# A linear attention, a top-2 expert layer and a gated layer on one core: other banks, other engines and other places for gathers

## The chip, the cores and the metric

The kernel runs on one core of a Trainium2 chip, as one program. The metric is the device time of a run in microseconds (us). The engines are TensorE (PE, matmuls; PEld its weight loads), VectorE (DVE), ScalarE (ACT), GpSimd (POOL) and SyncE (SP). In this kernel the matmuls write to PSUM, loads and the last stores are issued by SP, other stores by ACT, and gathers by a list of indices by POOL.

## The reference

```python
q_s = softmax(q, over its 64 columns);  k_s = softmax(k, over the 576 positions)
attn = q_s @ (k_s.T @ v)                       # 8 batches x 8 heads
x = attn as 4608 tokens x 512
noisy = x @ w_gate + log1p(exp(x @ w_noise)) * noise
top2 of 8 experts per token, weights = softmax of the two
x = sum over the two: weight * (relu(x @ w1[e]) @ w2[e])   # 512 -> 1024 -> 512
out = (((x @ m1) * (x @ m2)) @ w3) @ w_out
```

All values are float32. A product of two float32 values is made of three matmuls, since each operand is split in a high and a low part.

## The kernel before

**Attention and routing (`front`, L142).** A generator that handles 36 tiles of 128 tokens. Per tile `q_sub` (DVE maximum, POOL subtraction), `q_tr` (PE transpose), `q_exp` (ACT), `q_mm` (PE into the PSUM tile `pm`, 4 KB per partition, one buffer), `q_out` (DVE `qr`, ACT `xn` from `pm`, DVE `lp`, POOL `xt`, SP stores it to X). Between them `k_step` works on the keys of the next batch. `route` makes places and lists for groups of tokens: `onehots` (L371) turns a place into a tile number `jf` and a position `pf` (five DVE instructions), compares them with a ramp (`oa`, `ob`, DVE), multiplies `ob` by the token's tag (L402, POOL) and sums over PE. While the front is alone, its transposes take turns in four PSUM tiles of 2 KB (pools `ptr` and `pyy`, two each, called banks here), and the routing has two of its own (`phh`). At the mark "A" the first list `idxa` is there, and the experts' products start; from then on the rest of the front is drawn in between them (`hook_front`).

**Expert layer.** Work goes by units: a unit is two or three tiles of 128 gathered tokens of one expert. `product1` (eight PSUM tiles `ph`, each evacuated by ACT L738 and DVE L739 into `hT`) is followed by `product2` (a PSUM tile `py` for each 128 tokens; ACT L749 copies it to `y`, ACT issues the store to Y, L751). The tokens of the next unit are gathered by POOL from X, and turned by `transp`: in units 0 to 2 by a copy on POOL (`xr`, L122) and PE transposes, later by DVE alone. Unit 2 is the first whose gathers are cut in quarters (L137); the list of its indices is made at the end of unit 1. Until L872 a scheduler sets the order of instructions on each engine, by costs of its own; from there on the order is that of the code. Each engine works through its own queue in order.

**Last expert and gated layer.** `columns` (L877) after unit 5 prepares the places of every token: a clamp of `pos` on DVE (L879), then PE copies them to all partitions (`replicate`). Every tile of the gated layer needs two rows of Y per token, fetched by `gather2` (eight gathers on POOL) into the four buffers of `g2p`, weighted by ACT (L957) and DVE (L960) in `take`, and turned. `take` also starts the gather of the tile two further on. Tiles 0 and 1 are gathered before the last two units; `take(0)` to `take(2)` stand within these two units (events, L974 to L976), so gathers from Y are issued there between the stores to Y. The framework lets a store to Y wait for gathers from Y that stand before it in the code, and a gather wait for stores before it. The gated layer then runs 12 blocks of three tiles.

Of the kernel before, what the change touches and what calls it, by code (L numbers as in the profile page):

```python
# [24 lines left out]
D = NH * DH  # L25
# [13 lines left out]
CFB = {1: 0, 5: 1, 8: 2}  # L39
GROUPS = [(0, 9), (9, 15), (15, 18), (18, 26), (26, 32), (32, 35), (35, 36)]  # L40
# [3 lines left out]
def moe_chain_kernel(ctx, tc, q, kt, v0, v1, noise, wg, w1, w2, mw1, mw2, mw3t, mwo, out):  # L44
# [40 lines left out]
    def open_late():  # L85
        early.close()
        for name, bufs in (("w2", 4), ("ht", 1), ("xt", 2), ("xg", 3), ("y", 2)):
            late[name] = pool(main, name + "p", bufs, side="right", reuse_waits="tile")
    ptr = pool(main, "ptr", 2, space=PSUM)
    phh = pool(main, "phh", 2, space=PSUM)  # L90
    pyy = pool(main, "pyy", 2, space=PSUM)

# [9 lines left out]
    turns = {"ph": [phh], "py": [pyy]}  # L102
# [11 lines left out]
    def transp(src, xt, t, quarters):  # L114
        if quarters:
            pt = extra["xq"].tile([128, 4, 4, 32], F32, name="xq", tag="xq")
            V.transpose(out=pt, in_=src.rearrange("p (j c d) -> p c j d", j=4, c=4))  # L117
            pt = pt.rearrange("p c j t -> p c (j t)")
        else:
            pt = ptr.tile([128, 4, 128], F32, name="pt", tag="pt")  # L120
            rows = late["y"].tile([128, 4, 4, 32], F32, name="xr", tag="y")
            G.tensor_copy(out=rows, in_=by_chunk(src))  # L122
            for c in range(4):
                P.transpose(pt[:, c, :], rows[:, c].rearrange("p i d -> p (i d)"), ident)
        split(pt, xt[:, 0, :, 128 * t:128 * t + 128], xt[:, 1, :, 128 * t:128 * t + 128])
# [16 lines left out]
    def front(st):  # L142
# [12 lines left out]
        def bank(shape, route=False):  # L155
            if alone[0]:
                if route:
                    return phh.tile(shape, F32, name="rb", tag="ph")
                alone[1] += 1
                pl, tg = ((ptr, "pt"), (pyy, "py"))[alone[1] % 2]  # L160
                return pl.tile(shape, F32, name="fb", tag=tg)
            alone[1] += 1
            if alone[1] % 3 == 0:
                return pyy.tile(shape, F32, name="rb", tag="py")
            return ptr.tile(shape, F32, name="pt", tag="pt")
# [176 lines left out]
        def q_mm(i):  # L342
            pms[i] = pm = pmm.tile([128, 4, 256], F32, name="pm", tag="pm")
            b0, b1 = (i * 128) // S, (i * 128 + 127) // S
            for p in range(4):
                if b0 == b1:
                    P.matmul(pm[:, p, 0:162], eqs[i][:, p, :], tab[b0 % 3][:, p, :], start=True, stop=True)
                else:
                    P.matmul(pm[0:64, p, 0:162], eqs[i][:, p, 0:64], tab[b0 % 3][:, p, :], start=True, stop=True)
                    P.matmul(pm[64:128, p, 0:162], eqs[i][:, p, 64:128], tab[b1 % 3][:, p, :], start=True, stop=True)  # L350
# [20 lines left out]
        def onehots(i0, sl, cols, acc):  # L371
            n, kk = sl.shape[1], sl.shape[2]
            si = sm.tile([128, n, kk], I32, name="si", tag="si")
            V.tensor_copy(out=si, in_=sl)
            yield
            sj = sm.tile([128, n, kk], I32, name="sj", tag="sj")
            V.tensor_single_scalar(out=sj, in_=si, scalar=7, op=ALU.arith_shift_right)
            V.tensor_single_scalar(out=si, in_=si, scalar=127, op=ALU.bitwise_and)
            yield
            jf = sm.tile([128, n, kk], F32, name="jf", tag="jf")  # L380
            V.tensor_copy(out=jf, in_=sj)
            pf = sm.tile([128, n, kk], F32, name="pf", tag="pf")
            V.tensor_copy(out=pf, in_=si)
            yield
            per = 4 // kk
            for c0 in range(0, n, 2 * per):
                c1 = min(n, c0 + 2 * per)
                pl = bank([128, cols], True)
                for a in range(c0, c1, per):
# [11 lines left out]
                    obn = ob[:, 0:m].rearrange("p (n k) c -> p n k c", k=kk)  # L401
                    G.tensor_tensor(out=obn, in0=obn, in1=tag[:, i0 + a:i0 + z][:, :, None, None].to_broadcast(  # L402
                        [128, z - a, kk, cols]), op=ALU.mult)
# [26 lines left out]
        def route(gi):  # L430
# [32 lines left out]
            pr = bank([128, n, E], True)  # L463
# [51 lines left out]
            if i1 in (HT, NT):  # L515
                pc = bank([128, E], True)
# [201 lines left out]
    def xpose(u, t):  # L718
        if t == 0:
            xts[u] = late["xt"].tile([128, 2, 4, 384], F32R, name="xT", tag="xT")  # L720
        transp(xg.pop((u, t)), xts[u], t, u > na)
# [155 lines left out]
    def columns():  # L877

        V.tensor_scalar(out=pos, in0=pos, scalar1=float(E * ROWS - 1), scalar2=None, op0=ALU.min)  # L879
# [65 lines left out]
    def gather2(i):  # L945
        if i >= NT:
            return
        for k in range(2):
            y = extra["g2"].tile([128, D], F32, name="yg", tag="yg")
# [3 lines left out]
    def take(i):  # L953
# [11 lines left out]
        transp(y0, xts["g", b], t, True)  # L965
        gather2(i + 2)
# [6 lines left out]
    events[nu - 3, 7] = [w34_begin]  # L973
    events[nu - 2, 9] = [lambda: take(0)]  # L974
    events[nu - 1, 2] = [lambda: take(1)]
    events[nu - 1, 7] = [lambda: take(2), load_b]  # L976
    for u in range(na, nu):
# [4 lines left out]
        if u == na:  # L982
            turns["py"].append(ptr)
        if u == na + 3:
# [3 lines left out]
    for j in range(4):  # L988
        wscratch(("w", j), 20 + j, late["w2"])

    most = nc.values_load(nmax[0:1, 0:1], min_val=0, max_val=T)

    def gated():
# [3 lines left out]
        for b in range(nblk):  # L997
            xt = xts.pop(("g", b))
            pT = late["ht"].tile([128, 2, 8, 384], F32R, name="hT", tag="hT")
            for fb in range(8):  # L1000
# [13 lines left out]
                if b + 1 < nblk and fb in CFB:  # L1014
                    take(BT * (b + 1) + CFB[fb])
            for m in range(BT):
# [9 lines left out]
                if b + 1 < nblk and m + 8 in CFB:  # L1026
                    take(BT * (b + 1) + CFB[m + 8])

# [127 lines left out]
```

## Time and profile before

| | us |
|---|---|
| median of 3 runs (1743.0 to 1746.36) | 1745.32 |
| the profiled run | 1746.65 |
| its span, first to last instruction | 1744.7 |
| PE busy in it | 1665.7 |
| DVE / POOL / ACT busy | 886.3 / 690.7 / 572.5 |

The profile is of one execution. Its tables give busy time per engine, the span in slices with the clock that TensorE was granted (1.00 is 2.4 GHz, 0.50 is 1.2 GHz), what ended each idle time, and, for a chosen stretch, the instructions in order of time.

### The profile page before, as it was taken

What the parts mean: (1) busy time and instruction counts of PE and PEld (TensorE: products, weight loads), DVE (VectorE), ACT (ScalarE), POOL (GpSimd) and SP (SyncE); (2) the same over time, 40 slices, a digit from 0 to 9 for tenths busy, and PEclk for the clock granted to TensorE, in tenths of its full rate; (3) what the DMA queues carried; (4) which work ended last, traced back from release to release, by engine and by line L of the source; (5) the groups of instructions that cost most, each with busy time, mean ns of one, the idle gap of its engine ahead of it and who ended that gap; (6) DMA issues with size and microseconds to landing.
All of it is one profiled execution on the core that took longest, in us unless ns stands there. A gap on an engine that the chain in (4) does not pass through costs nothing. (4 is left out here: it accounts for less than half of the span.)

```text
span 1744.7 us, 26430 instructions
## 1 busy us (share of the span) xinstructions
PE 1665.7 (95%) x9903; PEld 1519.5 (87%) x9903; DVE 886.3 (51%) x2251; ACT 572.5 (33%) x1195; POOL 690.7 (40%) x706
## 2 busy tenths in 40 slices
PE   6887979989999999999999999899999999999998
PEld 5666868988989989899998988789999999999997
DVE  6699735766567575774767513233323233332321
ACT  6553322333233333332333312232223233232321
POOL 4456334414334143341443420544454454444500
PEclk9898989999999999999999999999999999999999
DMA  8875344535355253553545484521111111111100
GB/s 297 263 238 173 110 151 150 175 104 168 112 169 172 86 177 124 162 157 104 166 152 173 154 318 165 187 101 43 49 53 48 52 54 35 44 48 52 50 23 20
DMA packets 130060, 221.51 MB, mean 127 GB/s; under 512 B 18560, under 2 KB 65792, under 8 KB 126848
## 3 DMA queue, kind: packets, MB, share of 16 engines
q1 hardware_dynamic: 95040, 152.07, 26.7%
q0 software_dynamic: 19072, 39.88, 8.4%
q10 hardware_dynamic: 15808, 27.71, 4.3%
q8 instruction: 85, 1.39, 0.3%
q14 instruction: 55, 0.45, 0.1%
HBM read 152.22 MB, written 67.37 MB: 126 GB/s over the span
## 5 line engine op out<-in xcount | busy, mean ns | idle before, releaser
L98 PE MATMUL ph<-xT,w 128*128 128x384 f32 (+1 forms) x1792 | 576.2, 322 | 13.6 <-DVE hT L739 9.4
L99 PE MATMUL ph<-xT,w 128*128 128x384 f32 (+1 forms) x1792 | 574.6, 321 | 0.8 <-DVE xT L95 0.7
L100 PE MATMUL ph<-xT,w 128*128 128x384 f32 (+1 forms) x1792 | 574.0, 320 | 0.0
L137 POOL DMA_INDIRECT xg<-X,idxq x288 | 282.5, 981 | 467.7 <-DVE xq L117 395.3
L137 POOL DMA_INDIRECT yg<-Y,posq x288 | 295.0, 1024 | 364.9 <-DVE yg L960 209.0
L98 PEld LDWEIGHTS ph<-xT,w 128*128 128x128 f32 x1792 | 339.8, 190 | 18.6 <-DVE hT L739 11.8
L100 PE MATMUL py<-w,hT 128*128 128x512 f32 x904 | 353.0, 390 | 0.4
L99 PE MATMUL py<-w,hT 128*128 128x512 f32 x904 | 352.3, 390 | 0.0
L98 PE MATMUL py<-w,hT 128*128 128x512 f32 x904 | 352.2, 390 | 0.0
L99 PEld LDWEIGHTS ph<-xT,w 128*128 128x128 f32 x1792 | 339.4, 189 | 3.3 <-DVE xT L95 1.5
L100 PEld LDWEIGHTS ph<-xT,w 128*128 128x128 f32 x1792 | 339.5, 189 | 0.0
L100 PEld LDWEIGHTS py<-w,hT 128*128 128x128 f32 x904 | 169.7, 188 | 37.4 <-DVE hT L739 2.0
L99 PEld LDWEIGHTS py<-w,hT 128*128 128x128 f32 x904 | 169.7, 188 | 34.0
L98 PEld LDWEIGHTS py<-w,hT 128*128 128x128 f32 x904 | 169.7, 188 | 33.9
L1012 DVE TENSOR_TENSOR a<-a,ph 128x384 f32<-128x384 f32 x96 | 53.0, 552 | 281.6 <-PE ph L100 263.5
L739 DVE SCALAR_TENSOR_TENSOR hT<-ph,hT 128x256 fp32r<-128x256 f32 (+1 forms) x256 | 120.5, 474 | 103.4 <-ACT hT L738 100.4
L738 ACT ACTIVATE hT<-ph 128x256 fp32r<-128x256 f32 (+1 forms) x256 | 107.2, 426 | 158.1 <-PE ph L100 143.6
L95 DVE TENSOR_TENSOR xT<-xq,xT 128x512 fp32r<-128x512 f32 x108 | 74.8, 693 | 154.9 <-ACT xT L94 154.9
L749 ACT COPY y<-py 128x512 f32<-128x512 f32 x77 | 45.2, 587 | 258.0 <-PE py L100 214.4
L94 ACT CAST xT<-xq 128x512 fp32r<-128x512 f32 x108 | 67.0, 620 | 138.7 <-DVE xq L117 129.2
L94 ACT CAST hT<-a 128x384 fp32r<-128x384 f32 x96 | 49.4, 514 | 182.3 <-DVE a L1012 182.3
L95 DVE TENSOR_TENSOR w<-raw,w 128x1024 fp32r<-128x1024 f32 x72 | 88.8, 1236 | 11.7 <-ACT w L94 11.6
(203 smaller groups left out, 1529.5 us busy)
## 6 DMA issues: line engine op xcount, KB each, us to landing
raw<-in_w_dram SPq DMA_DIRECT2D x72, 512.0 KB, 4.1
w<-WS SPq DMA_DIRECT2D x24, 1024.0 KB, 6.6
WS<-hl SPq DMA_DIRECT2D x80, 256.0 KB, 2.8
Y<-y ACTq DMA_DIRECT2D x77, 256.0 KB, 2.5
k<-in_kt_dram SPq DMA_DIRECT2D x32, 288.0 KB, 4.4
q<-in_q_dram SPq DMA_DIRECT2D x36, 256.0 KB, 4.0
X<-xt SPq DMA_DIRECT2D x36, 256.0 KB, 2.4
out_dram<-y SPq DMA_DIRECT2D x36, 256.0 KB, 2.1
```

Of the source, the lines that this page charges most:

```text
L94: A.copy(out=hi, in_=src)
L95: V.tensor_tensor(out=lo, in0=src, in1=hi.bitcast(F32), op=ALU.subtract)
L98: P.matmul(ps, st_h, mv_h, start=first, stop=False)
L99: P.matmul(ps, st_h, mv_l, start=False, stop=False)
L100: P.matmul(ps, st_l, mv_h, start=False, stop=last)
L137: G.indirect_dma_start(out=dst[:, 128 * j:128 * j + 128], out_offset=None, in_=src[:].rearrange("t (i c) -> (t i) c", i=4), in_offset=bass ...
L738: A.activation(out=hT[:, 0, fb, :N], in_=ph[:, :N], func=AF.Relu)
L739: V.scalar_tensor_tensor(out=hT[:, 1, fb, :N], in0=ph[:, :N], scalar=0.0, in1=hT[:, 0, fb, :N].bitcast(F32), op0=ALU.max, op1=ALU.subtract)
L749: A.copy(out=by_chunk(y), in_=py.rearrange("p (c i d) -> p c i d", c=4, i=4))
L1012: V.tensor_tensor(out=a, in0=a, in1=ps, op=ALU.mult)
```

## The change

- PSUM: the two banks of `phh` are opened only when the expert layer starts; until then they hold `pm2`, a second tile for `q_mm`, which takes `pm` and `pm2` in turn. The routing's tiles join the four banks of the transposes.
- `onehots`: three float instructions on DVE instead of five with integers; the tags are multiplied by ACT, one instruction for each tile of tokens (54 in all), instead of by POOL (25).
- `transp` in units 0 to 2: the copy `xr` is made by ACT (units 0 and 1) or DVE (unit 2) instead of POOL.
- The clamp of `pos` moves from `columns` to the end of unit 2.
- `gather2(2)` moves ahead, to the middle of the last unit but one, into a freed weight buffer `raw`; `gather2(3)` and `gather2(4)` move behind the last store to Y; the first gated block takes its turns later (`CF0`).

```diff
+CF0 = {4: 0, 7: 1, 9: 2}
...
     def open_late():
         early.close()
+        turns["ph"].append(pool(main, "phh", 2, space=PSUM, side="right", reuse_waits="tile"))
...
-    phh = pool(main, "phh", 2, space=PSUM)
     pyy = pool(main, "pyy", 2, space=PSUM)
+    pm2 = pool(early, "pm2", 1, space=PSUM, side="right")
...
-    def transp(src, xt, t, quarters):
-        if quarters:
+    def transp(src, xt, t, straight):
+        if straight is None:
...
-            G.tensor_copy(out=rows, in_=by_chunk(src))
+            straight(out=rows, in_=by_chunk(src))
...
-        def bank(shape, route=False):
+        def bank(shape):
             if alone[0]:
-                if route:
-                    return phh.tile(shape, F32, name="rb", tag="ph")
...
-            pms[i] = pm = pmm.tile([128, 4, 256], F32, name="pm", tag="pm")
+            pms[i] = pm = (pm2 if alone[0] and i % 2 else pmm).tile([128, 4, 256], F32, name="pm", tag="pm")
...
-            si = sm.tile([128, n, kk], I32, name="si", tag="si")
-            V.tensor_copy(out=si, in_=sl)
-            yield
-            sj = sm.tile([128, n, kk], I32, name="sj", tag="sj")
-            V.tensor_single_scalar(out=sj, in_=si, scalar=7, op=ALU.arith_shift_right)
-            V.tensor_single_scalar(out=si, in_=si, scalar=127, op=ALU.bitwise_and)
-            yield
+
             jf = sm.tile([128, n, kk], F32, name="jf", tag="jf")
-            V.tensor_copy(out=jf, in_=sj)
+            V.tensor_scalar(out=jf, in0=sl, scalar1=1.0 / 128, scalar2=-0.49609375, op0=ALU.mult, op1=ALU.add)
+            yield
+            V.tensor_scalar(out=jf, in0=jf, scalar1=8388608.0, scalar2=-8388608.0, op0=ALU.add, op1=ALU.add)
+            yield
             pf = sm.tile([128, n, kk], F32, name="pf", tag="pf")
-            V.tensor_copy(out=pf, in_=si)
+            V.scalar_tensor_tensor(out=pf, in0=jf, scalar=-128.0, in1=sl, op0=ALU.mult, op1=ALU.add)
...
-                    obn = ob[:, 0:m].rearrange("p (n k) c -> p n k c", k=kk)
-                    G.tensor_tensor(out=obn, in0=obn, in1=tag[:, i0 + a:i0 + z][:, :, None, None].to_broadcast(
-                        [128, z - a, kk, cols]), op=ALU.mult)
+                    for j in range(z - a):
+                        obj = ob[:, kk * j:kk * j + kk]
+                        A.mul(out=obj, in_=obj, mul=tag[:, i0 + a + j:i0 + a + j + 1])
...
-        transp(xg.pop((u, t)), xts[u], t, u > na)
+        transp(xg.pop((u, t)), xts[u], t, None if u > na else V.tensor_copy if u == na else A.copy)
...
     def columns():
 
-        V.tensor_scalar(out=pos, in0=pos, scalar1=float(E * ROWS - 1), scalar2=None, op0=ALU.min)
...
+        if i == 2:
+            raw = rawp.tile([128, 2, D], F32, name="raw", tag="raw")
         for k in range(2):
-            y = extra["g2"].tile([128, D], F32, name="yg", tag="yg")
+            y = raw[:, k] if i == 2 else extra["g2"].tile([128, D], F32, name="yg", tag="yg")
...
-        gather2(i + 2)
+        if i >= BT:
+            gather2(i + 2)
...
+    events[nu - 2, 4] = [lambda: gather2(2)]
     events[nu - 2, 9] = [lambda: take(0)]
...
             turns["py"].append(ptr)
+            V.tensor_scalar(out=pos, in0=pos, scalar1=float(E * ROWS - 1), scalar2=None, op0=ALU.min)
...
         wscratch(("w", j), 20 + j, late["w2"])
+    gather2(3)
+    gather2(4)
...
+            turn_at = CFB if b else CF0
...
-                if b + 1 < nblk and fb in CFB:
-                    take(BT * (b + 1) + CFB[fb])
+                if b + 1 < nblk and fb in turn_at:
+                    take(BT * (b + 1) + turn_at[fb])
```

ACT's queue at the end of the last unit but one (steps 8 to 10 of unit `nu - 2`), before; `DMASW` are the signals of POOL's gathers, `DMAHW` those of other DMAs.

```order
L751 DMA Y_59<-y_12742 128x512 [waits DMAHW3_49,Activation_49]
L957 ACTIVATE yg_12363<-yg_12363,gwq_3515 128x128 x4
L94 CAST xT_12753<-xq_12754 128x4x128 [waits DVE_49]
L749 COPY y_12793<-py_12768 128x4x4x32 [waits DMAHW2_49,PE_49]
L751 DMA Y_59<-y_12793 128x512 [waits DMASW4_49,DMASW5_49,DMASW3_49,DMASW6_49,DMASW2_49,DMASW7_49,DMASW1_49,DMAHW5_49,DMASW0_49,Activation_49]
L738 ACTIVATE hT_12796<-ph_12797 128x256 [waits PE_49]
```

The same place in the changed kernel.

```order
L748 DMA Y_59<-y_12744 128x512 [waits DMAHW3_49,Activation_49]
L955 ACTIVATE yg_12356<-yg_12356,gwq_3508 128x128 x4
L96 CAST xT_12755<-xq_12756 128x4x128 [waits DVE_49]
L746 COPY y_12785<-py_12760 128x4x4x32 [waits DMAHW2_49,PE_49]
L748 DMA Y_59<-y_12785 128x512 [waits Activation_49]
L735 ACTIVATE hT_12788<-ph_12789 128x256 [waits PE_49]
```

The store of the third tile no longer waits for any gather; the instructions around it are the same.

POOL's queue from the end of unit 1 on, before (`xg` from `idx` are unit 2's gathers, those from `idxq` the next units').

```order
L402 TENSOR_TENSOR ob<-ob,tag 128x160 x2
L709 DMA xg<-X,idx 128x512 x3
L122 COPY xr<-xg 128x512
L137 DMA xg<-X,idxq 128x128 x4
L122 COPY xr<-xg 128x512
L137 DMA xg<-X,idxq 128x128 x4
L122 COPY xr<-xg 128x512
L137 DMA xg<-X,idxq 128x128 x40
```

DVE's queue in the changed kernel, where the three copies now stand: the end of unit 1 and the first evacuation of unit 2.

```order
L736 SCALAR_TENSOR_TENSOR hT<-ph,hT 128x256
L124 COPY xr<-xg 128x512 x2
L97 TENSOR_TENSOR xT<-pt,xT 128x4x128 x2
L124 COPY xr<-xg 128x512
L97 TENSOR_TENSOR xT<-pt,xT 128x4x128
L736 SCALAR_TENSOR_TENSOR hT<-ph,hT 128x384
```

The copies left POOL, where four gathers stood between each two of them, and stand on DVE with only the evacuations of the same tiles between.

DVE's queue between unit 5 and unit 6, before: conversion of the gated layer's weights (L628 to L635), then `columns`.

```order
L645 TENSOR_TENSOR hl<-mf,u 128x256
L628 TENSOR_SCALAR ex<-cr 128x256
L630 TENSOR_SCALAR b_4790<-cr 128x256
L633 SCALAR_TENSOR_TENSOR b_4790<-cr,b_4790 128x256
L635 SCALAR_TENSOR_TENSOR mf<-ex,b_4790 128x256
L879 TENSOR_SCALAR pos<-pos 128x72
L880 TENSOR_SCALAR posq<-py,quart 128x288
```

The same place in the changed kernel.

```order
L642 TENSOR_TENSOR hl<-mf,u 128x256
L625 TENSOR_SCALAR ex<-cr 128x256
L627 TENSOR_SCALAR b_4784<-cr 128x256
L630 SCALAR_TENSOR_TENSOR b_4784<-cr,b_4784 128x256
L632 SCALAR_TENSOR_TENSOR mf<-ex,b_4784 128x256
L876 TENSOR_SCALAR posq<-py,quart 128x288
```

The clamp of `pos` (L879) is gone from here; it now stands at the end of unit 2.

## Rows read from the trace of the kernel before

**Rows 1.** The page, busy time of each engine over the span.

```profile
PE 1665.7 (95%) x9903; PEld 1519.5 (87%) x9903; DVE 886.3 (51%) x2251; ACT 572.5 (33%) x1195; POOL 690.7 (40%) x706
```

**Rows 2.** Windows, end of unit 5 to product2 of unit 6; a later product1.

```profile
368.10:393.45 25.35, 20.63 (x161) 20.46 (x161) 17.73 (x42) 9.00 (x16) 3.78 (x4) 0.87 0.49 146
487.35:504.58 17.23, 17.15 (x98) 16.82 (x96) 14.34 (x31) 9.01 (x16) 3.77 (x4) 1.00 0.60 191
```

**Rows 3.** Windows: unit 5, last unit, gated blocks 0 and 1.

```profile
345.90:368.10 22.20, 22.20 (x145) 19.97 (x143) 11.10 (x30) 6.31 (x14) 6.45 (x7) 1.00 0.27 82
...
1130.56:1185.08 54.52, 51.62 (x265) 48.47 (x264) 16.17 (x34) 14.81 (x34) 26.62 (x27) 0.97 0.32 113
1185.08:1235.38 50.30, 50.30 (x266) 47.44 (x265) 16.26 (x34) 14.91 (x34) 24.81 (x25) 1.00 0.17 48
1099.39:1130.56 31.17, 24.17 (x146) 22.08 (x145) 7.97 (x20) 7.37 (x20) 19.36 (x20) 0.89 0.58 210
```

**Rows 4.** Timeline of ACT, last two units: start, length, in brackets idle before.

```profile
1089.32 0.33 ACTq L751 DMA_DIRECT2D Y<-y  x1
...
1111.26 0.94 ACT L738 ACTIVATE hT<-ph 128x256 fp32r<-128x256 f32 x3 [11.08 <-DMA yg<-Y,posq]
...
1140.22 0.58 ACT L749 COPY y<-py 128x512 f32<-128x512 f32 x1 [14.32 <-DMA yg<-Y,posq]
```

**Rows 5.** Timeline of POOL and DVE, last two units.

```profile
1104.31 0.94 POOL L137 DMA_INDIRECT yg<-Y,posq  x1 [0.30 <-issue]
...
1070.12 1.23 DVE L95 TENSOR_TENSOR w<-raw,w 128x1024 fp32r<-128x1024 f32 x1 [0.38 <-ACT w L94]
```

**Rows 6.** Chain of waits: start, length, the last gather's landing.

```profile
1133.78 5.91 DMA yg<-Y,posq
```

**Rows 7.** Timeline of PE between units 5 and 6.

```profile
372.83 1.19 PE L132 MATMUL py<-pos,ident 128*32 128x72 f32 x32 [4.72 <-DVE pos L879]
```

**Rows 8.** Timelines of POOL, ACT, DVE and PE between units 1 and 2.

```profile
248.10 0.61 POOL L122 COPY xr<-xg 128x512 f32<-128x512 f32 x1 [12.63 <-DMA Y<-y]
...
249.46 0.59 ACT L94 CAST xT<-pt 128x512 fp32r<-128x512 f32 x1 [0.62 <-PE pt L124]
...
250.08 0.69 DVE L95 TENSOR_TENSOR xT<-pt,xT 128x512 fp32r<-128x512 f32 x1 [9.36 <-ACT xT L94]
...
248.76 0.66 PE L124 MATMUL pt<-ident,xr 128*128 128x128 f32 x4 [0.55 <-POOL xr L122]
254.38 1.12 PE L124 MATMUL pt<-ident,xr 128*128 128x128 f32 x4 [4.96 <-POOL xr L122]
...
261.79 0.69 PE L98 MATMUL ph<-xT,w 128*128 128x384 f32 x1 [0.68 <-ACT xT L94]
```

**Rows 9.** Windows of the front: alone, start of the products, units 0 and 1.

```profile
62.00:130.00 68.00, 54.04 (x560) 45.53 (x560) 60.94 (x249) 41.97 (x91) 32.63 (x34) 0.95 0.76 247
130.00:153.40 23.40, 15.93 (x154) 12.83 (x150) 21.44 (x42) 7.74 (x13) 18.77 (x20) 0.72 0.70 222
153.40:248.90 95.50, 88.81 (x680) 77.52 (x681) 69.07 (x279) 32.05 (x68) 34.45 (x38) 1.00 0.40 138
```

**Rows 10.** Waits from 40 to 153: engine, releaser, us in total, times, longest.

```profile
PE pm L347 <- DVE lp L360: 12.7, 8, 4.0
...
DVE qr L355 <- PE pm L347: 7.3, 8, 1.4
```

**Rows 11.** Groups by line, 60 to 153.4, DVE and POOL: busy, mean ns.

```profile
L377 DVE TENSOR_SCALAR sj<-si 128x12 int32<-128x12 int32 (+3 forms) x6 | 2.2, 361 | 0.0
...
L402 POOL TENSOR_TENSOR ob<-ob,tag 128x320 f16<-128x320 f16 (+4 forms) x10 | 6.7, 673 | 4.9 <-DVE ob L398 2.4 <-DVE si L374 1.4 <-DVE qr L355 0.9
```

**Rows 12.** Timeline of DVE, one instruction at two times.

```profile
89.24 0.15 DVE L269 TENSOR_SCALAR ks<-ks 128x4 f32<-128x4 f32 x1
...
135.09 3.25 DVE L269 TENSOR_SCALAR ks<-ks 128x4 f32<-128x4 f32 x1
```

**Rows 13.** Waits from 153 to 249.

```profile
POOL ob L402 <- DVE ob L398: 19.1, 8, 8.3
```

More of the change, by code (lines that the diff above doesn't have):

```diff
@@ L100, in mm3 @@
         P.matmul(ps, st_l, mv_h, start=False, stop=last)
-    turns = {"ph": [phh], "py": [pyy]}
+    turns = {"ph": [], "py": [pyy]}
     def bank_of(kind, shape):
@@ L372, in onehots @@
             n, kk = sl.shape[1], sl.shape[2]
-            si = sm.tile([128, n, kk], I32, name="si", tag="si")
-            V.tensor_copy(out=si, in_=sl)
+            jf = sm.tile([128, n, kk], F32, name="jf", tag="jf")
+            V.tensor_scalar(out=jf, in0=sl, scalar1=1.0 / 128, scalar2=-0.49609375, op0=ALU.mult, op1=ALU.add)
             yield
-            sj = sm.tile([128, n, kk], I32, name="sj", tag="sj")
-            V.tensor_single_scalar(out=sj, in_=si, scalar=7, op=ALU.arith_shift_right)
-            V.tensor_single_scalar(out=si, in_=si, scalar=127, op=ALU.bitwise_and)
+            V.tensor_scalar(out=jf, in0=jf, scalar1=8388608.0, scalar2=-8388608.0, op0=ALU.add, op1=ALU.add)
             yield
-            jf = sm.tile([128, n, kk], F32, name="jf", tag="jf")
-            V.tensor_copy(out=jf, in_=sj)
             pf = sm.tile([128, n, kk], F32, name="pf", tag="pf")
-            V.tensor_copy(out=pf, in_=si)
+            V.scalar_tensor_tensor(out=pf, in0=jf, scalar=-128.0, in1=sl, op0=ALU.mult, op1=ALU.add)
             yield
@@ L387, in onehots @@
                 c1 = min(n, c0 + 2 * per)
-                pl = bank([128, cols], True)
+                pl = bank([128, cols])
                 for a in range(c0, c1, per):
@@ L462, in route @@
             yield
-            pr = bank([128, n, E], True)
+            pr = bank([128, n, E])
             P.matmul(pr, upper, m, start=True, stop=False)
@@ L515, in route @@
             if i1 in (HT, NT):
-                pc = bank([128, E], True)
+                pc = bank([128, E])
                 P.matmul(pc, onesb, run, start=True, stop=True)
@@ L964, in take @@
             xts["g", b] = late["xt"].tile([128, 2, 4, 384], F32R, name="xT", tag="xT")
-        transp(y0, xts["g", b], t, True)
-        gather2(i + 2)
+        transp(y0, xts["g", b], t, None)
+        if i >= BT:
+            gather2(i + 2)
     def load_b():
@@ L1025, in gated @@
                 nc.sync.dma_start(out=out[r:r + 128, :], in_=y)
-                if b + 1 < nblk and m + 8 in CFB:
-                    take(BT * (b + 1) + CFB[m + 8])
+                if b + 1 < nblk and m + 8 in turn_at:
+                    take(BT * (b + 1) + turn_at[m + 8])
     gated()
```

## The prediction

> **What bounds the kernel now.** I read the busy times of the page first: PE is busy 1665.7 of 1744.7 us [rows 1]. The change leaves the number of matmuls as it is, so it can win only where PE stands (79 us in all) or runs at the lower clock. Next the slices, to find these places, and windows cut at them. Three lie in the experts' part and one is the front. Between unit 5 and unit 6, 25.35 us pass until product1 is over, at a mean clock of 0.87; the same product1 elsewhere takes 17.23 [rows 2]. The last unit takes 31.17 us and the first gated block 54.52, where equal work takes 22.20 and 50.30 [rows 3]. Between units 1 and 2, PE has only transposes to do for 13 us [rows 8]. In the front DVE is the fullest engine: 60.94 of 68 us while the front is alone, 21.44 of 23.4 until the products start; after that PE is, 88.81 of 95.5 [rows 9]. Last I read at each place what ended the wait, and then the queues of the change there.
>
> **The stores to Y.** In the last unit but one, `take(0)` issues `gather2(2)` ahead of the third store to Y, and this store waits for it. Eight gathers at 0.94 + 0.30 us make 9.9 us [rows 5], and the landing follows. ACT's queue is in order, so behind the store stand the evacuations of the last unit's product1: ACT is idle 11.08 us, until the gathers' data is there, and again 14.32 us behind the first store of the last unit [rows 4]. PE runs out of PSUM tiles. Price: 31.17 - 22.20 = 8.97 us and 54.52 - 50.30 = 4.22 us, together 13.2; both windows show a mean clock below 1, 0.89 and 0.97, so the sum holds the half clock after the stalls too [rows 3].
> In the changed kernel `gather2(2)` waits for a weight buffer, which is free when its split is done: 1070.12 + 1.23 = 1071.4 on the clock of the profile, if it is the first of this unit's splits [rows 5]. Then 9.9 us of issue and at most 5.9 of landing (the longest that I see [rows 6]) end at 1087.2, ahead of the first store to Y at 1089.3 [rows 4]. If the buffer is that of the fourth split, three `ph` tiles of 2.15 us (17.23 / 8) later, ACT is held 4.4 us inside product2; a `py` tile takes PE (50.30 - 2 x 17.23) / 3 = 5.3 us, and four of them take turns: nothing. No gather stands between the later stores.
> What is late next are `gather2(3)` and `gather2(4)`, which wait for the last store. Let T be the start of the gated layer. The copy of 0.58 and the store end by T + 0.6 + 0.3 + 5.9 = T + 6.8, sixteen gathers of 1.24 are issued by T + 16.7 and T + 26.6, and landed by T + 22.6 and T + 32.5. A gated block's first part is two times the 17.23 of rows 2; `take(3)` stands after five eighths of it, T + 21.5, `take(4)` at its end, T + 34.5. In the worst case ACT is 1.1 us late at the first, and PE has four `ph` tiles to bridge that. So I take the whole 13.2; bounds 9 (the first stall alone) and 13.2.
>
> **The clamp of the places.** PE stands 4.72 us for the clamp of `pos` [rows 7], which queues on DVE behind weight conversions. The 25.35 us hold a product1 (17.23) and two copies of the places, 2 x 0.8 us at full clock (the 1.19 of the row is at half clock). The rest, 25.35 - 17.23 - 1.6 = 6.5 us, is stall and half clock. The clamp now stands three units earlier; PE's copies wait only for banks, and `posq` and `gwq` are read much later. The conversions now hold DVE beside unit 6's first tile, which four `ph` tiles hide. I take 6.5; bounds 4.7 and 6.5.
>
> **The copies between units 1 and 2.** POOL makes `xr` at 248.10 when a store to Y has landed, and then issues four gathers before each further copy: PE's second transposes start at 254.38, unit 2 at 261.79 [rows 8]. On DVE no gather stands between. The first copy starts at 248.10 as before and takes at most the 0.69 of DVE's row. Transposes 0.66 to 249.45; the second copy waits for them, 250.1; transposes 250.8; ACT 0.59 to 251.4, DVE 0.69 to 252.1; third copy 252.8; transposes at half clock 1.12 to 253.9; ACT to 254.5. Unit 2 starts at 254.6 instead of 261.79: 7.2 us. [...] Bounds: 5 (each copy waits for a further store of 2 us) and 7.5. The conversions' first load is tied to unit 2's first tile, and the stop that it makes later moves along.
>
> **The front.** Four effects, none of which the trace shows alone.
> The integer steps: ten calls drop two DVE instructions each, six calls by 153. At 0.15 us free of POOL [rows 12] to 0.36 [rows 11] that is 1.8 to 4.3 us of DVE; I take 3.
> The second `pm`: DVE waited 7.3 us for PE's `pm`, and PE 12.7 for DVE to empty it [rows 10]. DVE is the fuller engine, so 0 to 7.3; DVE needs the time for other work in most of them, I take 2.5.
> POOL's multiplications: 6.7 us by 153 [rows 11]. A DVE instruction of 0.15 us took 3.25 beside POOL's work [rows 12], so taking some away frees DVE: 0 to 6.7, I take 2.5.
> Against it: ACT gets 54 small multiplications and five copies. None is longer than the 0.59 of a 128x512 row, so at most 35 us of ACT, of which the front alone has 42 of 68 busy and units 0 and 1 32 of 95.5 [rows 9]. Their waits are worse than their work: POOL waited 19.1 us for `ob` in units 0 and 1 [rows 13], and ACT has evacuations queued behind. The routing now shares four banks. Below nothing is excluded, as both only add waits; from 0 to 19, and I take 2, near the low end, since PE then has the front's own matmuls between the products.
> Front: 3 + 2.5 + 2.5 - 2 = 6 us, bounds +18 (gains all, cost none: 4.3 + 7.3 + 6.7) and -17.
> By the Trainium skill (SBUF — State Buffer, Who interferes with whom), DVE and GpSimd share a pair of ports that whoever comes first holds for its whole instruction; rows 12 agree with it. By that rule all 6.7 us would come back, and the front would win 10.
>
> **Edits that cost nothing.** The later turns of the first block (`CF0`) only move work inside a block in which PE is full; `ph`'s later opening leaves PE's order in the experts as it is. The last block's end is untouched.
>
> **Sum.** 13.2 + 6.5 + 7.2 + 6 = 32.9 us off the profiled run's 1746.65 gives 1713.7. The median of the runs shown is 1.3 lower than the profiled one, so 1712.4.
>
> **Rivals.**
> The front frees DVE fully (17 in 100): +18 instead of 6, 1700. For it: DVE is 90% full there. Against it: `xn` and `xt` have one buffer each, and loads keep the DMA share at 0.76 [rows 9].
> The front wins nothing, or loses up to 15 us, by waits in ACT's queue (16 in 100): 1718 to 1733, some 1724 in the middle.
> The gathers' stall comes back (4 in 100): `gather2(3)` lands late by more than four `ph` tiles cover, as 5.91 us is from a stretch with fewer weights loading. From T + 30 on each us counts in full; with the 13.2 lost, 1725.6.
> Slower (3 in 100): ACT takes over POOL's waits in units 0 and 1. The place is ACT's queue ahead of L738, with two `ph` tiles there. If the 19.1 us and all 35 us of new work delayed PE, the front would lose 54 instead of winning: 1746.65 - 26.9 + 54 - 1.3 = 1772. It decides from 27 us of such delay on. Against it: ACT is idle for two thirds of that stretch.
>
> **How the numbers follow.** Forecast 60 in 100, alone 1706 to 1718. The range takes in the bounds of the front and most of the rivals: 1697 to 1730. About 0.2% (3.5 us) is what a measurement can tell; only the last rival and the worst of the second end there or above. Faster 0.95, within it 0.02, slower 0.03.
>
> **What would show it.** The stores: no ACT idle time ended by a gather from Y in the last two units, and these at 22.2 and 50.3 us. The clamp: no PE wait for `pos`, product1 over within 19 us of unit 5's end. The copies: unit 2 starts within 6 us of unit 1's end. The front: unit 0's first product before 150 us, and PE's idle time in units 0 and 1 not above 6.7 us. It is wrong if ACT shows waits for `ob` with PE idle behind them, or if the first gated block still takes over 52 us.

## The result and the profile after

The changed kernel takes 1722.72 us (median of 4 runs, 1715.42 to 1725.67) against 1744.73 us before: ratio 0.9868, 95% interval 0.9835 to 0.9900. A second group of runs gave 0.9831 (0.9809 to 0.9853). It is faster by 22 to 27 us, where I had forecast 32.9 off the profiled run. The profiled run's span is 1721.8 us, 22.9 under that of before.

The page first: PE has the same work as in [rows 1] in a shorter span, POOL has less, ACT more.

```profile
PE 1666.7 (97%) x9903; PEld 1518.0 (88%) x9903; DVE 881.1 (51%) x2234; ACT 590.8 (34%) x1254; POOL 669.0 (39%) x673
```

Windows of the changed kernel (stretch, length, busy time of PE, PEld, DVE, ACT and POOL, granted clock, DMA share, GB/s): unit 5, end of unit 5 to product2 of unit 6, the last unit, gated blocks 0 and 1; then two windows of the front as in [rows 9], and units 0 and 1.

```profile
343.95:366.06 22.11, 22.11 (x148) 19.94 (x151) 11.13 (x30) 6.31 (x14) 6.35 (x7) 1.00 0.27 81
366.06:383.86 17.80, 17.80 (x160) 17.70 (x161) 16.50 (x39) 8.79 (x16) 3.78 (x4) 1.00 0.66 202
1089.80:1111.91 22.11, 22.11 (x145) 20.21 (x144) 8.11 (x20) 7.61 (x20) 0.00 (x0) 1.00 0.71 254
1111.91:1162.21 50.30, 50.30 (x266) 47.44 (x265) 16.37 (x34) 15.02 (x34) 31.13 (x32) 1.00 0.37 123
1162.21:1212.50 50.29, 50.29 (x265) 47.44 (x264) 16.26 (x34) 14.93 (x34) 30.83 (x31) 1.00 0.20 56
...
62.00:130.00 68.00, 53.48 (x540) 44.35 (x540) 60.62 (x243) 42.97 (x105) 32.61 (x30) 0.94 0.79 249
130.00:153.40 23.40, 18.82 (x155) 15.72 (x154) 17.34 (x34) 11.62 (x25) 13.24 (x12) 0.67 0.70 224
155.57:250.83 95.26, 88.92 (x675) 76.22 (x674) 66.18 (x269) 41.35 (x96) 20.42 (x19) 1.00 0.40 139
```

Against [rows 2, 3] the last unit is 31.17 - 22.11 = 9.06 shorter, block 0 4.22, and the way from unit 5 to product2 of unit 6 25.35 - 17.80 = 7.55. The front is different: DVE is as full as in [rows 9] while the front is alone; after 130 us DVE has become emptier (21.44 to 17.34) and PE fuller (15.93 to 18.82), and yet unit 0's first product, the start of the last row, is at 155.57 instead of 153.37.

The two places in the experts that went as expected. PE between units 5 and 6 (start, length, instruction): both copies of the places follow unit 5 at once, where [rows 7] has a wait of 4.72.

```profile
365.98 0.71 PE L134 MATMUL py<-pos,ident 128*32 128x72 f32 x32
366.51 0.68 PE L134 MATMUL py<-gw,ident 128*32 128x72 f32 x32
```

POOL's gathers from Y: the first and the last of `gather2(2)`, now into `raw`, and the first of `gather2(3)`.

```profile
1062.02 0.95 POOL L139 DMA_INDIRECT raw<-Y,posq  x1 [21.11 <-DVE w L97]
...
1071.36 0.94 POOL L139 DMA_INDIRECT raw<-Y,posq  x1 [0.30 <-issue]
...
1121.47 0.94 POOL L139 DMA_INDIRECT yg<-Y,posq  x1 [49.17 <-DVE a L1016]
```

ACT in the last unit and block 0: a store to Y goes out with no wait in front of it, the evacuations after it wait for PE alone (compare [rows 4]; the copy and the store of 1112 are the last of the experts), and the first weighting of `take(3)` (L955) stands behind no gap.

```profile
1090.61 0.33 ACTq L748 DMA_DIRECT2D Y<-y  x1
...
1092.80 0.39 ACT L735 ACTIVATE hT<-ph 128x256 fp32r<-128x256 f32 x1 [1.01 <-PE ph L102]
...
1112.11 0.59 ACT L746 COPY y<-py 128x512 f32<-128x512 f32 x1 [4.86 <-PE py L102]
1112.73 0.33 ACTq L748 DMA_DIRECT2D Y<-y  x1
...
1134.39 1.28 ACT L955 ACTIVATE yg<-yg,gwq 128x128 f32<-128x128 f32 x4
```

Units 1 and 2: unit 1's last product ends at 250.83, and unit 2 starts 8.47 us later (13.57 before, when it ended at 248.22). On DVE no gather stands between the copies any more (the quartered ones from `idxq`, which stood there on POOL, are those of unit 3 on; unit 2's own rows come whole, by `idx`), but the first copy waits for the landing of the store of 246.00: 252.92 - 246.00 = 6.9 us after its issue.

```profile
246.00 0.33 ACTq L748 DMA_DIRECT2D Y<-y  x1
```
```profile
252.92 0.43 DVE L124 COPY xr<-xg 128x512 f32<-128x512 f32 x1 [8.13 <-DMA Y<-y]
254.10 0.43 DVE L124 COPY xr<-xg 128x512 f32<-128x512 f32 x1 [0.75 <-PE pt L126]
...
256.92 0.47 DVE L124 COPY xr<-xg 128x512 f32<-128x512 f32 x1
```
```profile
259.30 0.69 PE L100 MATMUL ph<-xT,w 128*128 128x384 f32 x1 [0.68 <-ACT xT L96]
```

By places: 9.06 + 4.22 + 7.55 + (13.57 - 8.47) = 25.9 won in the experts, against 2.2 lost until unit 0 starts, 0.4 in units 0 and 1 and 0.4 in units 2 to 5: 22.9. What is short of the forecast is the front, with 6 expected, and the copies.

### The profile page after: what moved, and what is told of

The parts are those of the page before. It is cut to its first block, busy times and chain, and to the rows that moved or that the text cites. A ratio compares the mean times of both kernels' runs of the same rounds, so it can differ in the third digit from the quotient of the medians.

```text
span 1721.8 us, 26420 instructions
## 1 busy us (share of the span) xinstructions
PE 1666.7 (97%) x9903; PEld 1518.0 (88%) x9903; DVE 881.1 (51%) x2234; ACT 590.8 (34%) x1254; POOL 669.0 (39%) x673
## 5 line engine op out<-in xcount | busy, mean ns | idle before, releaser
L139 POOL DMA_INDIRECT yg<-Y,posq x280 | 285.5, 1020 | 329.6 <-DVE yg L958 173.7
```

Source lines behind the costliest of these rows:

```text
L139: G.indirect_dma_start(out=dst[:, 128 * j:128 * j + 128], out_offset=None, in_=src[:].rearrange("t (i c) -> (t i) c", i=4), in_offset=bass ...
```

## The experiments

Each was timed in 5 rounds and profiled once. Runs of one group share a chip and the runs of the kernel before. The third group fell on another chip, on which the kernel before took 1765.3 instead of 1747: its times are compared with each other only. "Lists" is the moment at which `idxa` is ready; the next three columns run from there to unit 0's first product, over units 0 and 1, and from unit 1's end to unit 2's first product. The last is the way from the lists to product2 of unit 6, which leaves out how long the front took until the lists. Two profiles of one kernel differ in it by 2.6 us (before) and 3.8 us (changed), so less than 4 us in this column says nothing.

| kernel | median us | ratio (95%) | lists | to unit 0 | units 0, 1 | to unit 2 | lists to unit 6 |
|---|---|---|---|---|---|---|---|
| before, first profile | 1744.7 | | 129.92 | 23.45 | 94.85 | 13.57 | 263.5 |
| changed, first profile | 1722.7 | 0.9868 | 129.44 | 26.13 | 95.26 | 8.47 | 254.4 |
| after_again | 1720.6 | 0.9831 (0.9809 to 0.9853) | 130.04 | 25.90 | 93.94 | 7.66 | 250.6 |
| front_back | 1723.1 | 0.9855 (0.9836 to 0.9874) | 130.81 | 28.27 | 95.70 | 5.23 | 252.6 |
| experts_back | 1751.7 | 1.0024 (1.0010 to 1.0039) | 131.27 | 26.14 | 96.05 | 14.42 | 266.9 |
| xr_pool | 1723.3 | 0.9859 (0.9840 to 0.9879) | 130.59 | 28.98 | 92.58 | 7.71 | 253.1 |
| before_again | 1746.2 | 0.9995 (0.9981 to 1.0008) | 129.00 | 23.60 | 94.84 | 12.25 | 260.9 |
| front_back2 | 1718.8 | 0.9837 (0.9811 to 0.9864) | 129.65 | 23.38 | 95.19 | 4.74 | 246.7 |
| xq_rows | 1720.6 | 0.9835 (0.9809 to 0.9861) | 136.65 | 26.07 | 97.06 | 3.29 | 249.1 |
| pm_one | 1714.6 | 0.9803 (0.9778 to 0.9828) | 133.26 | 19.96 | 93.11 | 4.90 | 242.4 |
| shared_one | 1754.2 | 0.9941 (0.9923 to 0.9959) | 136.23 | 23.05 | 93.48 | 5.40 | 247.7 |
| one_pm_pool | 1748.4 | 0.9909 (0.9888 to 0.9930) | 129.34 | 24.50 | 92.41 | 5.57 | 247.3 |
| one_pm_int | 1749.5 | 0.9911 (0.9894 to 0.9929) | 129.73 | 21.60 | 97.75 | 4.88 | 247.8 |
| best | 1742.2 | 0.9878 (0.9857 to 0.9899) | 128.10 | 19.74 | 94.35 | 3.29 | 241.9 |

The way from the lists to unit 0 is the steadiest measure: four profiles with the changed kernel's front give 25.90 to 26.14, three with that of before 23.38 to 23.60. The lists themselves come up to 7 us later in some executions of one front (129.44 and 136.65; 128.10 and 133.26 for best and pm_one). The granted clock goes with it only in part: between 90 and 130 us it is 0.81 in xq_rows, against 0.93 in the changed kernel's first profile, but 0.91 in best and 0.90 in pm_one.

Behind unit 6 the edits of the front change nothing: from its product2 to the end, the seven profiles with the changed experts that are not of the third group take 1338 us. On the third group's chip all four take 1368 to 1370.

**First group: is it the front?**

after_again, without an edit. 

> The changed kernel once more, as the base of the other runs of this call and to see how far its front varies from one execution to the next (its four times so far reach from 1715.4 to 1725.7 us). If the front is steady and costs 2 us (theory 1), unit 0 starts again near 155.6 us and the median is near 1722.7. If the start moves by several us between executions (theory 2), the profile shows another start, the difference of the spans is the difference of the starts, and the 2 us of one profile mean little. The last unit (22.2), the first gated block (50.3) and unit 6 (17.8 from unit 5's end to product2) are the same under both.

Unit 0 starts at 155.94 and the last unit, block 0 and unit 6 are the same to 0.1 us: the front lags steadily, theory 1.

experts_back, the three places in the experts as before:

```diff
-            V.tensor_scalar(out=pos, in0=pos, scalar1=float(E * ROWS - 1), ...)   # behind unit 2
+        V.tensor_scalar(out=pos, in0=pos, scalar1=float(E * ROWS - 1), ...)       # in columns()
-        if i >= BT:
-            gather2(i + 2)
+        gather2(i + 2)
-    events[nu - 2, 4] = [lambda: gather2(2)]
-    gather2(3)
-    gather2(4)
+            turn_at = CFB
+    ... xr of unit 2: G.tensor_copy
```

> The changed kernel with its three changes in the experts undone: the gathers of rows of Y and the turns of block 0 in the old order, the clamp of pos back in columns(), xr of unit 2 on POOL again. The front's edits stay. From the windows of the two traces the experts' part was worth 13.3 + 7.5 + 5 = 25.8 us, so this is 1748.5 if the rest of the change is the -2.5 that the traces show (theory 1), that is slightly slower than the kernel before (1744.7). By my forecast the front wins 6 and this is 1739. Last unit 31, first block 54.5, and 25 us from unit 5 to product2 of unit 6 should come back.

It is 31 us slower than after_again, slower than the kernel before, and the old waits are back: ACT's two gaps (11.14 and 14.50, ended by gathers from Y), the last unit at 30.98, block 0 at 55.14, 24.92 to unit 6, 14.42 to unit 2. So the three edits are worth all of the gain, and the front's edits together lose.

```profile
1115.99 0.94 ACT L735 ACTIVATE hT<-ph 128x256 fp32r<-128x256 f32 x3 [11.14 <-DMA yg<-Y,posq]
...
1144.90 0.59 ACT L746 COPY y<-py 128x512 f32<-128x512 f32 x1 [14.50 <-DMA yg<-Y,posq]
```

front_back, the four edits of the front undone, but with one `yield` more than before in `onehots`:

```diff
-            pms[i] = pm = (pm2 if alone[0] and i % 2 else pmm).tile(...)     # and phh, route as before
+            pms[i] = pm = pmm.tile(...)
-            ... jf, pf by three float instructions
+            ... si, sj, jf by integers
+            V.tensor_copy(out=jf, in_=sj)
+            yield                                                            # not there before
-                        A.mul(out=obj, in_=obj, mul=tag[...])
+                    G.tensor_tensor(out=obn, in0=obn, in1=tag[...], op=ALU.mult)
-    ... else A.copy)
+    ... else G.tensor_copy)
```

> The changed kernel with the four edits of the front undone: integer steps, one pm tile and the routing's own two banks, the tag multiplied by POOL, xr of units 0 and 1 copied by POOL. The three changes in the experts stay. As I forecast (the front's edits win 6 us) it is 6 slower than the changed kernel: 1729, unit 0 at about 161 by the changed kernel's clock. If the front's edits win nothing or lose (theory 1, from the two traces: unit 0 at 153.4 before, 155.6 after) it is 1719 to 1722, and unit 0 starts at 153 to 154. In both cases the gain that is left against the kernel before is that of the experts, 23 to 27 us, ratio 0.985 to 0.987.

It missed both theories: unit 0 starts at 159.08. The extra turn alone, against front_back2, costs 28.27 - 23.38 = 4.9 us to unit 0 and 5.9 to unit 6: a turn without any work in it lets the scheduler set another order on every engine. On PE all 80 matmuls of a batch's tables (`v,ek`) now stand behind both waits for `lp`, right ahead of the queries and of unit 0's transposes, which start at 155.55; in front_back2 68 of them run ahead of the first wait and all 80 ahead of the second. Banks, tiles and engines are the same in both.

```profile
141.95 2.50 PE L348 MATMUL pm<-tab,eqT 128*128 128x162 f32 x8 [2.79 <-DVE lp L361]
...
145.05 2.99 PE L265 MATMUL pt<-v,ek 128*64 128x64 f32 x38 [0.33 <-DVE lacc L411]
148.50 3.39 PE L265 MATMUL pt<-v,ek 64*64 64x64 f32 x42
```

xr_pool:

```diff
-        transp(..., None if u > na else V.tensor_copy if u == na else A.copy)
+        transp(..., None if u > na else V.tensor_copy if u == na else G.tensor_copy)
```

> The changed kernel with one edit undone: xr of units 0 and 1 copied by POOL again, not by ACT. Theory 3: in the changed kernel the third xr of unit 0 starts at 153.26 only because ACT's queue holds it behind the exponentials of a query tile (151.41, which wait 5.3 us for pm) and two casts; POOL, which stood idle from 147.9 to 154.5, would make it as soon as its rows have landed, at about 151.5. Then unit 0 starts 1.5 to 2 us earlier (153.6 to 154.1) and the kernel is at 1720.5 to 1721. If the start is set by PE's own queue (the attention's matmuls, 143.2 to 151.2) it stays at 155.6 and the time at 1722.7.

Theory 3 is wrong. On POOL the third copy waits 3.97 us for the transposes of the first, which PE reaches later still (155.70, against 151.17 in the changed kernel), and is made at 156.84; the start goes from 155.9 to 159.6.

**Second group: which edit of the front?**

before_again, without an edit. 

> The kernel before once more, for a second profile of its front. Theory 2 (the start of the products moves by some us between executions of one kernel) expects the start of unit 0 elsewhere than at 153.4, up to 159, with the lists ready at 129 to 131. Theory 1 (the front's edits cost 2 us) expects 153.4 within 0.5 us, as both profiles of the changed kernel show 155.6 and 155.9. Time 1745 to 1748 under both.

152.60, within 0.8 us of the first profile, and 23.60 from the lists: theory 2 is out for this stretch.

front_back2, against front_back:

```diff
             V.tensor_copy(out=jf, in_=sj)
-            yield
```

> The changed kernel with its four edits of the front undone, as front_back, but with the integer steps in the same turns as before (front_back had one turn more in them, by which the order of PE's instructions in the front was neither the one nor the other). PE's order is now that of the kernel before to the last instruction. If the front's edits lose 2 us (theory 1), unit 0 starts at 153.4 and the time is 2 to 3 us under the changed kernel, 1718 to 1720. If they win 6 us as forecast: 1727 to 1729, a ratio of 0.989. If they win nothing, as what the front gains is lost again in the wait between units 1 and 2: 1721 to 1723.

Unit 0 is at 153.03, and the time is the 1718 to 1720 of theory 1. On the same chip the kernel before took 1746.7: the three edits in the experts alone win 27.9 us (my terms for them: 13.2 + 6.5 + 7.2 = 26.9). The copies win 13.57 - 4.74 = 8.8 here. The first copy starts 3.2 us after the issue of the store at 243.43, where it took 4.7 in the first profile of before and 3.4 in before_again; against this one, with nearly the same landing, they win 7.5:

```profile
246.59 0.43 DVE L123 COPY xr<-xg 128x512 f32<-128x512 f32 x1 [5.90 <-DMA Y<-y]
```

pm_one:

```diff
-        turns["ph"].append(pool(main, "phh", 2, space=PSUM, side="right", ...))
-    pm2 = pool(early, "pm2", 1, space=PSUM, side="right")
+    phh = pool(main, "phh", 2, space=PSUM)          # from the start; the routing's own banks
-            pms[i] = pm = (pm2 if alone[0] and i % 2 else pmm).tile(...)
+            pms[i] = pm = pmm.tile(...)
```

> The changed kernel with one edit of the front undone: one pm tile, ph's banks open from the start, the routing in its own two banks. My forecast gave the second pm 2.5 us (bounds 0 to 7.3) and the shared banks a small loss: 1723 to 1725. If the waits for pm only move to other places (theory 1) the time is that of the changed kernel within 2 us, and unit 0 starts at 153 to 156. If the second pm is what the front gains from, it is 1726 to 1730 with PE's waits for lp up by 3 us and more before unit 0.

All three expectations missed: it is faster, 1714.6, 32.1 under the kernel before. The edit that I had credited with a gain costs. The windows from the lists to unit 0 of before, the changed kernel, pm_one and shared_one:

```profile
129.92:153.37 23.45, 15.98 (x154) 12.88 (x150) 21.49 (x43) 7.73 (x14) 18.74 (x20) 0.71 0.71 223
```
```profile
129.44:155.57 26.13, 21.00 (x171) 17.43 (x170) 19.73 (x42) 14.35 (x29) 14.39 (x13) 0.69 0.66 213
```
```profile
133.26:153.22 19.96, 15.88 (x152) 13.23 (x151) 18.32 (x41) 12.50 (x26) 12.45 (x12) 0.76 0.79 253
```
```profile
136.23:159.28 23.05, 17.34 (x176) 13.54 (x174) 19.60 (x46) 15.85 (x33) 16.02 (x14) 0.92 0.63 197
```

In the changed kernel PE is the full engine here (21.0 of 26.1 at a clock of 0.69), with 17 matmuls more in the stretch than before. PE's rows show which stand where. Before, all 80 matmuls `v,ek` of a batch's tables run ahead of PE's long wait for `lp`, and the transposes of `xr` follow the queries' `pm` at 149.78:

```profile
132.41 2.72 PE L264 MATMUL rb<-v,ek 128*64 128x64 f32 x54
...
136.05 0.97 PE L264 MATMUL rb<-v,ek 128*64 128x64 f32 x14
...
140.30 1.11 PE L264 MATMUL rb<-v,ek 128*64 128x64 f32 x12
...
146.32 0.88 PE L347 MATMUL pm<-tab,eqT 128*128 128x162 f32 x2 [4.03 <-DVE lp L360]
...
149.78 0.79 PE L124 MATMUL pt<-ident,xr 128*128 128x128 f32 x4
```

In the changed kernel PE waits first and has these 80 behind it, at a granted clock of 0.50, shortly ahead of the transposes:

```profile
138.07 0.97 PE L347 MATMUL pm<-tab,eqT 128*128 128x162 f32 x4 [3.73 <-DVE lp L360]
...
142.36 0.69 PE L264 MATMUL pt<-v,ek 128*64 128x64 f32 x6
...
143.22 5.69 PE L264 MATMUL pt<-v,ek 128*64 128x64 f32 x74
148.85 2.53 PE L347 MATMUL pm<-tab,eqT 128*128 128x162 f32 x8
151.17 1.58 PE L126 MATMUL pt<-ident,xr 128*128 128x128 f32 x8
```

With one `pm` and own banks 46 of them lie ahead of the wait (2.30) again, the other 34 behind it:

```profile
137.42 1.58 PE L265 MATMUL rb<-v,ek 64*64 64x64 f32 x30
141.31 1.06 PE L348 MATMUL pm<-tab,eqT 128*128 128x162 f32 x6 [2.30 <-DVE lp L361]
...
142.82 2.77 PE L265 MATMUL rb<-v,ek 128*64 128x64 f32 x34
```

xq_rows:

```diff
-            rows = late["y"].tile([128, 4, 4, 32], F32, name="xr", tag="y")
+            rows = extra["xq"].tile([128, 4, 4, 32], F32, name="xq", tag="xq")   # unit 2 alone
```

> The changed kernel with xr of unit 2 in the two buffers of the later xq and not in those of y. In the changed kernel the first copy waits until a store to Y of 246.00 has landed (252.92), and unit 2 starts 8.5 us after unit 1's end (7.7 in the second profile). If this landing sets the start, the copies are made before unit 1 ends, the transposes follow its last product at once, and the third copy, which waits for the first transposes, sets the start: some 4 us after unit 1's end, 4 us faster than the changed kernel, 1717 to 1718. If the gathered rows of X land as late as the store, the start stays 7.7 to 8.5 us behind, and the time is that of the changed kernel, 1721 to 1723.

The landing of the store is what held the copies: two are made at 246.36, unit 1 ends at 259.78, and unit 2 starts 3.29 us behind it instead of 7.7 to 8.5. The time does not show it: 0.9835 on its chip is after_again's 0.9831 on another, and its profiled run had its lists 7 us late. Inconclusive on the time.

```profile
259.62 1.03 PE L129 MATMUL pt<-ident,xq 128*128 128x128 f32 x8
...
263.07 0.44 PE L100 MATMUL ph<-xT,w 128*128 128x384 f32 x1 [0.67 <-ACT xT L96]
```

**Third group: sharing or the second tile, and what the other two edits win**

shared_one, against the changed kernel:

```diff
-            pms[i] = pm = (pm2 if alone[0] and i % 2 else pmm).tile(...)
+            pms[i] = pm = pmm.tile(...)
```

> The changed kernel with the attention on one pm tile, but everything else of that edit left: ph's banks opened late and the routing in the four shared banks (two PSUM banks stand empty). One pm tile with the routing in banks of its own was 1714.6, the changed kernel 1720.6 to 1722.7. If the loss of 6 us comes from the sharing (the routing takes turns in the banks that the attention's tables wait for), this is as slow as the changed kernel, 1720 to 1723, with 25 to 26 us from the lists to unit 0's first product. If it comes from the second pm tile itself (the queries run ahead and push the tables' 80 matmuls behind them), this is 1714 to 1716.

It is slow: 12 us behind best (2 of them behind unit 6), 5 to 6 behind the two kernels with own banks that lack one more gain each. With the 32 us that this chip costs behind unit 6 taken off, its median is 1722, an estimate from the profiles: that of the changed kernel (1720.6 to 1722.7), and 7 over pm_one. So the sharing, with the later opening of `ph` that is part of the edit, costs about what the whole edit costs. All 80 matmuls of the tables stand right ahead of the first transposes here too, in 3.58 us, as the granted clock was 1.00 there:

```profile
150.24 3.58 PE L264 MATMUL pt<-v,ek 128*64 128x64 f32 x80
153.75 0.66 PE L126 MATMUL pt<-ident,xr 128*128 128x128 f32 x4
```

A cost of the second tile beside that is not shown. From the lists to unit 6 the changed kernel takes 2.9 to 6.7 us more than shared_one, and shared_one 5.3 more than pm_one, but the lists of shared_one came late in its profile (136.23), which this column leaves out. What goes with the second tile throughout is the wait to unit 2: 7.7 to 8.5 in the three kernels with two `pm` tiles and the copies on DVE in `y`, and at most 5.6 in the six with one.

Over all profiles the place of the 80 goes with the way to unit 0: it takes 23.05 to 28.98 us in the seven in which all of them start 12.5 us or more after the lists, and 19.74 to 24.50 in the seven in which 46 or more start within 7 us of the lists.

one_pm_pool, against pm_one:

```diff
-                        A.mul(out=obj, in_=obj, mul=tag[...])
+                    G.tensor_tensor(out=obn, in0=obn, in1=tag[...], op=ALU.mult)
-    ... else A.copy)
+    ... else G.tensor_copy)
```

> The kernel with one pm tile and the routing's own banks (1714.6), and the tag multiplied and xr of units 0 and 1 copied by POOL again: of the front's edits only the float steps are left. The kernel with all four edits undone was 1718.8. If the float steps win the 3 us that I forecast and the move to ACT wins little (2.5 less 2), this is 1715 to 1716. If the move to ACT is what won, it is 1718 to 1719.

one_pm_int, against pm_one:

```diff
-            ... jf, pf by three float instructions
+            ... si, sj, jf, pf by five integer ones and casts
```

> The kernel with one pm tile and the routing's own banks (1714.6), with the integer steps back, in their old turns: of the front's edits only the move from POOL to ACT is left. By my forecast (3 us for the float steps, 0.5 for the move) 1718 to 1719. If the move to ACT is what won the 4.2 us, 1715.

Neither alone shows a gain: from the lists to unit 6 both take 247 to 248, as does the kernel with none of the four edits (246.7), while both together take 242.4, 4.3 less, little over what two profiles of one kernel differ by. The medians say the same: front_back2 and pm_one on one chip differ by 4.2, and the two kernels here are 6 to 7 behind best, of which its edit at unit 2 was to be 1.6. The two times here (1748.4 and 1749.5) are the same within their intervals. The forecasts for the parts missed; that the one for the sum (3 + 2.5 less some of the 2) held is in part luck.

best, pm_one with the diff of xq_rows. 

> One pm tile and the routing's own banks, and xr of unit 2 in the buffers of xq: the two edits that the runs so far speak for, together. With xq's buffers unit 2 started 3.3 us after unit 1's end instead of 7.7 to 8.5; with one pm tile this wait is already down to 4.9, so 1.6 us are left to win: 1713, ratio 0.979. If the landing of the store is no longer what holds the copies with one pm tile, it stays at 1714.6.

The wait to unit 2 is 3.29, as expected. It is the fastest of its group by 6 us and more and reaches unit 6 soonest of all from the lists (241.9). It beats the kernel before by 1.2% on its chip (23 us by the medians), where pm_one on the other beat it by 32: on the third chip the kernel before is some 19 us slower, and those with the changed experts lose 30 to 32 behind unit 6. Against the changed kernel the nearest comparison is shared_one, 12 us behind. That it beats pm_one is not shown, as they ran on different chips.

## Why the prediction came out as it did

The time, 1722.7, lies in the range of 1697 to 1730, but outside the 1706 to 1718 that I gave the forecast alone: the range held because it took in a front that loses.

**The stores to Y: right.** 9.06 + 4.22 = 13.28 for 13.2. `gather2(2)` began when the first split of the unit freed `raw`, as read from [rows 5], and was through before the first store. One assumption was off: `gather2(3)` began at T + 9.6 (1121.47 - 1111.91), not by T + 6.8. Its row names a DVE instruction of block 0 as releaser, but POOL's wait ended at 1120.7, when the last store landed, 8.0 us after its issue; I had taken 5.9 as the longest landing. It cost nothing, since ACT reached `take(3)` at T + 22.5 with no gap.

**The clamp: right, 7.5 for 6.5.** The 1.6 us for the two copies at full clock were 1.07, as the second overlaps the first.

**The copies: mechanism right, size 5.1 for 7.2** (the lower bound was 5). From the first copy to unit 2 it took 6.4 us, my 6.5. What failed was "the first copy starts at 248.10 as before": it waits for a store's landing, 3.2 us in front_back2, 4.7 before and 6.9 in the changed kernel. Where the landing was alike (before_again and front_back2) the gain was 7.5. Why the store lands later with two `pm` tiles was not settled.

**The front: wrong, and this is the step that failed.** For the second `pm` I wrote 0 to 7.3 and took 2.5, for the shared banks a part of 2 lost. Together they cost: by the ratios 0.9803 and 0.9831 to 0.9868, 5 to 11 us, and on one chip pm_one is 6.0 under xq_rows, which has both, with no run of one among those of the other. I read the two waits at `pm` [rows 10] as time that a second tile gives back, and priced the sharing as a wait for a bank. Neither is how it acts. The second tile did take DVE's wait for PE's `pm` from 7.3 to 2.6 us, but DVE then waited 5.4 us (11.6 in after_again; neither profile of before has such a wait) for POOL's `xt`, the next tile with one buffer, and PE still waited 9.7 for `lp`. In the changed kernel, 40 to 153 us:

```profile
DVE qr L355 <- POOL xt L363: 5.4, 4, 1.9
...
DVE qr L355 <- PE pm L347: 2.6, 3, 1.8
```

And a scheduler sets the order here: with other banks it put the tables' 80 matmuls behind a wait instead of ahead of it. The diff does not show this, the order does, and I had compared the orders for the last units only. That the edit to the banks loses is shown by pm_one and shared_one; that another order alone, with the same banks and tiles, costs about 5 us to unit 0 is shown by front_back. That it is the place of the 80 and nothing else in the order is read from the rows, not tried by itself. Why the scheduler chose so was not tried, and no run has a second tile without shared banks. The bounds took in the loss (down to -17), the middle did not. The rest of the forecast, 32.9 less the 0.5 for these two, is what pm_one won: 32.1. That is in part luck, as two of its terms, 3 and 2.5 us, did not come one by one.

**POOL's work beside DVE.** [rows 12] showed one DVE instruction of 0.15 us stretched to 3.25. In pm_one, with the tags on ACT, one that takes 0.68 elsewhere still took 3.40, while POOL does the front's other work (`xt` from 137.37, then `q`):

```profile
137.56 3.40 DVE L391 TENSOR_TENSOR oa<-iob,pf 128x512 f16<-128x512 bf16 x1
138.37 2.04 POOL L330 TENSOR_TENSOR q<-q,qmx 128x512 f32<-128x512 f32 x2
```

So the 6.7 us of POOL's work did not come back: 23.4 to 21.6 to unit 0 for the move alone (front_back2 to one_pm_int, one profile each), and nothing by unit 6. The Trainium skill (SBUF — State Buffer, Who interferes with whom) names the shared ports; the stretch agrees with it, the 10 us that I drew from it for the front does not.

**The rivals.** "The front wins nothing, or loses up to 15" came true (1718 to 1733, middle 1724; 16 in 100). Not by its mechanism: ACT waits 10.2 us for `ob` in units 0 and 1, POOL had waited 19.1, and PE's idle time there is 95.26 - 88.92 = 6.3, under the 6.7 named. So the slower rival is out too. No ACT gap ends at a gather from Y in the last two units.

**The signs named.** The stores and the clamp met theirs; unit 2 within 6 us of unit 1's end did not (8.47); unit 0 before 150 did not (155.57).

## What to carry to other kernels

Where a scheduler sets the order, compare PE's order at every place that an edit touches, above all ahead of the first instruction of the next stage: an extra turn without work moved this front by 5 us, as much as any edit in it. A second buffer is not worth the wait that it removes if the wait moves on to the next tile with one buffer, or if it is paid with banks in which others take their turns. Places that follow the order of the code (a store behind a gather, a clamp behind conversions) could be priced from windows to about 1 us; the copies, which waited for a store to land, only to 2.

## What the runs showed of the hardware

On the chip of the third group all four kernels lose 30 to 32 us behind unit 6, at the same places. The gated blocks 0 and 1 took 57.9 and 58.9 us in shared_one, 59.8 and 56.4 in one_pm_pool, 58.2 and 57.7 in one_pm_int, 62.1 and 50.3 in best; with the changed experts on the other chips both take 50.30. PE stands still in the middle of a tile, its gaps have no releaser ("issue"), and ACT and DVE stand still with it, at a DMA share of 0.13 to 0.21. On the other chips PE has no such gap behind unit 6. What it was is open. PE's windows and rows there, in shared_one:

```profile
1145.00:1150.00 5.00, 5.00 (x30) 5.00 (x29) 1.11 (x2) 0.51 (x1) 3.84 (x4) 1.00 0.21 56
...
1155.00:1161.00 6.00, 3.07 (x10) 2.57 (x10) 0.55 (x1) 0.18 (x1) 1.89 (x3) 0.67 0.13 33
```
```profile
1155.90 0.34 PE L102 MATMUL ph<-xT,w 128*128 128x384 f32 x1 [2.11 <-issue]
...
1158.73 0.48 PE L100 MATMUL ph<-xT,w 128*128 128x384 f32 x1 [1.77 <-issue]
```

A store of 256 KB to Y at one and the same place, before unit 2, let the first copy go 3.2, 4.7 or 6.9 us after its issue: 3.4 and 4.7 in two profiles of the kernel before, 6.6 and 6.9 in two of the changed one. The last store of the experts landed 7.7 to 8.1 us after its issue in the changed kernel, front_back2, xq_rows and pm_one.
